# The first 35 microseconds of a linear-attention and MLP kernel: which queue loads what first, and in which order TensorE works

## The chip, the cores and the metric

The kernel runs on one core of a Trainium2 chip. A core has five engines that run at the same time, each in the order of its own instruction list: TensorE (PE, matrix products), VectorE (DVE), ScalarE (ACT), GpSimd (POOL) and SyncE (SP). Data comes from and goes to the chip's main memory by DMA transfers; SP, ACT and POOL issue them, each into a queue of its own, and 16 DMA engines carry all queues. Engines wait for each other and for transfers through semaphores. The metric is the time of one execution on the chip in microseconds (us); the median of three runs before the change is 657.64 us (657.43 to 659.58).

## The reference

Inputs are q, k and v of shape (4, 8, 768, 64) (batch, heads, positions, width of a head), a decay `lam` for each head, and the weights `w_in` (512 x 2048) and `w_out` (2048 x 512). The first half is linear attention with decay, in blocks of positions; the second half is an MLP with the activation h - tanh(h):

```python
intra = np.einsum('bhic,bhjc->bhij', qb, kb) * Dmask[None]
intra = np.einsum('bhij,bhjd->bhid', intra, vb)
inter = np.einsum('bhid,bhde->bhie', qb * lam_pow[None], kv_state)
out[:, :, sl] = intra + inter
kv_state = lam_block[None, :, None, None] * kv_state + np.einsum('bhsd,bhse->bhde', kb_dec, vb)
...
x = np.ascontiguousarray(attn_out.transpose(0, 2, 1, 3)).reshape(B * S, H * D)
h = x @ w_in
g = h - np.tanh(h)
return (g @ w_out).astype(np.float32)
```

`Dmask` holds `lam ** (i - j)` for i >= j and 0 otherwise, and `kb_dec` is k times `lam ** (block - 1 - position)`.

## The kernel before

The kernel works through the 768 positions in six groups of 128 positions (`NG`, `BLK`), each group with all four batches, so that one group makes 512 rows for the MLP. A *chunk* is one group of one batch: chunk (0, 2) is group 0, batch 2. For each chunk the kernel needs q, k and v as tiles of 128 positions by 8 heads by 64 (256 KB each).

The part around the change is group 0, where no state has to be read yet. For each of its four chunks:

- `load_natural` (line 153) issues the loads of q, k and v. All q go on SP's queue. Of group 0, the k of batches 0 and 1 goes on ACT's queue and everything else on POOL's (line 164).
- `att_transpose` (line 371) transposes q and k on TensorE (line 384, tiles `tp`), four products each, and ScalarE copies each result out of the accumulator memory (line 386, `qt` and `kt`).
- `att_scores` (line 393) makes the scores, eight products (line 400, tiles `sp`); VectorE multiplies them with the decay mask `whole` (line 407, tile `ss`, two instructions). `whole` is made once by eight scans on VectorE (line 110) out of `lam_all`, the decay of all heads, and the identity, which POOL writes.
- `att_decay` (line 428) scales k in place on VectorE (line 430).
- `first_out` (line 444) multiplies masked scores with v, eight products (line 451, tiles `op`). `first_tokens` (line 455) copies the outputs of two batches to `xt` on ScalarE (line 458): this is the input of the MLP.
- `kv_products` (line 432) and `first_state` (line 462) make the state that group 1 reads, from the scaled k and v of two batches.

The weights arrive as 64-bit words, in blocks. `load_weights` (line 254) issues the load of a raw block, `weights` (line 264) rounds the next ones (`round_block`, line 322): three passes on ScalarE (lines 332 to 334) and two on VectorE (lines 336, 337). Raw blocks have four buffers, so a block's load has to wait for the rounding of the block four places ahead of it. `ready["may"]` bounds how many raw blocks may be loaded so far; each `w_in` block has 512 KB, and blocks 2 and 3 of every four are loaded in two halves (line 250).

`up_plain` (line 887) is the first MLP product (tiles `h`, line 895). In the beginning it is used as an iterator, `unit`: `steps(unit, 2)` issues the next two of its steps, so that its products stand between the attention's.

`idle_products(n)` (line 358) issues n products of a tile of zeros into an unused bank of the accumulator memory. Their result is not used; they fill TensorE's time.

Order is written out by hand in this stretch: nearly every instruction is kept in program order (`tied`, `keep_in_program_order`), and the lines 969 to 1017 say which piece comes after which. `held(op, engines...)` (line 961) makes the next load on each of the named queues wait for `op`; what stands behind that load in the same queue waits with it. Before the change three places use it: loads of chunk (0, 2) wait for the masked scores of batch 0 (line 971), raw block 2 for the masked scores of batch 1 (line 978), and chunk (0, 3) with what follows for the first copy to `xt` (line 984).

In the built program each transfer of the hardware queues (SP and ACT) takes one of eight completion semaphores in turn, POOL's transfers have their own eight. A transfer waits, in its queue, until the earlier one with the same semaphore has landed.

Of the kernel before, what the change touches and what calls it, by code (L numbers as in the profile page):

```python
# [24 lines left out]
def kernel(  # L25
# [32 lines left out]
    nc = tc.nc  # L58
    B, H, S, D = q.shape
# [33 lines left out]
    lam_all = const.tile([128, H], F32)  # L93
    fwd = const.tile([128, NP, BLK], F32)
    nc.vector.memset(fwd[:, 0, :], 0.0)
    nc.gpsimd.dma_start(out=lam_all, in_=bass.AP(tensor=lam.tensor, offset=lam.offset, ap=[[0, 128], [1, H]]))
    make_identity(nc, ident)


# [53 lines left out]
    def load_natural(g, b, names):  # L153
        for name, src, bufs in (("q", q, 2), ("k", k, 3), ("v", v, 4)):
            if name in names:
                if (g, b, name) in ((0, 2, "q"), (0, 3, "q"), (0, 3, "k")):
                    x = opool.tile([128, H, D], F32, name=f"{name}_nat", tag="o")
                else:
                    x = (qpool if name == "q" else io).tile([128, H, D], F32, name=f"{name}_nat", tag=name, bufs=bufs)
                rows = src[b, :, ts(g, BLK), :].rearrange("h s d -> s h d")  # L160
                if name == "q":
                    parts = [(nc.sync, x, rows)]
                elif g == 0:
                    parts = [(nc.scalar if name == "k" and b < 2 else nc.gpsimd, x, rows)]
                else:
                    parts = [(nc.sync, x[ts(1 - t, HALF), 4:8], rows[ts(t, HALF), 4:8]) for t in range(2)]
                    parts.insert(0, (nc.sync, x[:, 0:4], rows[:, 0:4]))
                for eng, to, of in parts:
                    op = tc.keep_in_program_order(eng.dma_start(out=to, in_=of))  # L169
                    if begin.get(eng) is not None:  # L170
                        wait_for(op, begin.pop(eng))
                raw[g, b][name] = x
# [81 lines left out]
    def load_weights(n):  # L254

        while ready["loaded"] < min(n, ready["may"]):
            if moe_w_in.dtype != F32:
                raw64 = stage.tile([128, 2, 256], I64, name="raw64", tag="raw64", bufs=WAHEAD)
                block = blocks[ready["loaded"]]
                load_block(nc.gpsimd if ready["loaded"] in range(NU * KI, NU * KI + 4) else nc.sync, raw64, *block, True)  # L260
                wraw[ready["loaded"]] = raw64
            ready["loaded"] += 1
# [79 lines left out]

    for b in range(B):
        raw[0, b] = {}
    for b in (0, 1):
        load_natural(0, b, "qk")
    ready["may"] = 1
    load_weights(1)
    for b in (0, 1):
        load_natural(0, b, "v")  # L350
    ready["may"] = 2
    load_weights(2)
    at["loaded"] = B


# [2 lines left out]
    def idle_products(n, first=False):  # L358

        for _ in range(n):  # L360
            tied(not first, nc.tensor.matmul(out=idle[:, 0:128], lhsT=fwd[:, 0, :], rhs=fwd[:, 0, :], start=True, stop=True))
# [31 lines left out]
    def att_scores(g, bs):  # L393
        for b in bs:
            qt, kt, _ = tr[g, b]
            if g == 0:
                sp = [bank("sp", "att", 4).rearrange("s (p i) -> s p i", p=NP) for _ in range(2)]
                for p in range(NP):
                    for j in range(2):
                        tied(True, nc.tensor.matmul(out=sp[j][:, p, :], lhsT=kt[ts(j, 64), p, :],  # L400
                                                    rhs=qt[ts(j, 64), p, :], start=True, stop=True))
                if b % 2 == 0:
                    sc[0, "half"] = wst.tile([128, 8, 256], F32, name="ss", tag="w").rearrange(
                        "s (b j x) c -> s b j (x c)", b=2, j=2).rearrange("s b j (p i) -> s b j p i", p=NP)
                ss = sc[0, "half"][:, b % 2]
                for j in range(2):
                    op = tied(True, nc.vector.tensor_tensor(ss[:, j], sp[j], whole[:, j], op=AL.mult))
                sc[g, b] = ss
                continue

            sp = [bank("sp", "att", 4)[:, 0:6 * HALF].rearrange("s (x i) -> s x i", x=6) for _ in range(2)]
            for p in (0, 2, 1, 3):
                x, r = p % 2, p // 2
                for j in range(2):
                    kj, qj = kt[ts(j, 64), p, :], qt[ts(j, 64), p, :]

                    k0, k1 = (kj[:, ts(t if r == 0 or g >= GB else 1 - t, HALF)] for t in range(2))
                    tied(g != 1, nc.tensor.matmul(out=sp[j][ts(r, HALF), x:3 + p:2 + p - x, :], lhsT=k0,  # L418
                                                  rhs=qj.rearrange("d (t i) -> d t i", t=2), start=True, stop=True))
                    tied(g != 1, nc.tensor.matmul(out=sp[j][ts(1 - r, HALF), 2 + p, :], lhsT=k1,  # L420
                                                  rhs=qj[:, HALF:BLK], start=True, stop=True))
            ss = work.tile([128, 2, 6, HALF], F32, name="ss", tag="ss")
            for j in range(2):
                op = tied(g != 1, nc.vector.tensor_tensor(ss[:, j], sp[j], mask[:, j], op=AL.mult))
            sc[g, b] = ss
        return op

    def att_decay(g, b):
        kp = raw[g, b]["k"].rearrange("s (p j) d -> s p j d", j=2)
        return tied(g != 1, nc.vector.tensor_tensor(kp, kp, bwd if g > 0 else bwd_first, op=AL.mult))  # L430

    def kv_products(g, bs):

        kv = bank("kv", *(("yb", 1) if g >= GB else ("z", 1) if (g, bs) == (0, (0, 1)) else ("att", 4))).rearrange("d (b p e) -> d b p e", b=2, p=NP)
        for n, b in enumerate(bs):
            kd, vn = raw[g, b]["k"], raw[g, b]["v"]
            for p in range(NP):
                for j in range(2):
                    tied(g == 0, nc.tensor.matmul(out=kv[ts(j, 64), n, p, :], lhsT=kd[:, 2 * p + j, :],
                                                  rhs=vn[:, 2 * p + j, :], start=n == 0 and p == 0, stop=True,  # L440
                                                  skip_group_check=True))
        return kv

    def first_out(b):
        n, half = b % 2, b // 2
        if n == 0:
            reads[0, half] = [bank("op", "att", 4).rearrange("d (p b s) -> d p b s", p=2, b=2) for _ in range(2)]
        ops, ss, vn = reads[0, half], sc.pop((0, b)), raw[0, b]["v"]
        for p in range(NP):
            for j in range(2):  # L450
                tied(True, nc.tensor.matmul(out=out_dst(ops, n, p, j), lhsT=vn[:, 2 * p + j, :], rhs=ss[:, j, p, :],
                                            start=n == 0 and p % 2 == 0, stop=n == 1 and p % 2 == 1,
                                            skip_group_check=True))
# [507 lines left out]
    def held(op, *engines):  # L961
        begin.clear()
        begin.update({eng: op for eng in engines})

    def more_raw(n):
        ready["may"] = n
        load_weights(n)

    att_transpose(0, (0,))
    idle_products(3)  # L970
    held(att_scores(0, (0,)), nc.sync, nc.gpsimd)
    load_natural(0, 2, "qk")
    att_decay(0, 0)
    att_transpose(0, (1,))
    idle_products(2)
    first_out(0)
    att_decay(0, 1)
    held(att_scores(0, (1,)), nc.sync)
    more_raw(3)
    kv = kv_products(0, (0, 1))  # L980
    idle_products(2)
    weights(1)
    first_out(1)
    held(first_tokens(0)[0], nc.sync, nc.gpsimd)
    load_natural(0, 3, "qk")
    load_natural(0, 2, "v")
    more_raw(4)
    load_natural(0, 3, "v")
    ready["may"] = len(blocks)
    idle_products(6)  # L990
    unit = up_plain(0, [(i, c + 10 * a) for c in (11, 12) for i in range(KI) for a in range(2)])
    steps(unit, 2)
    weights(2)
    idle_products(4)
    att_transpose(0, (2,))
    steps(unit, 2)
    weights(3)
    att_scores(0, (2,))
    att_decay(0, 2)
    idle_products(6)  # L1000
    att_transpose(0, (3,))
    steps(unit, 2)
    weights(4)
    att_scores(0, (3,))
    first_out(2)
    att_decay(0, 3)
    idle_products(4)
    first_out(3)
    first_tokens(1)
    first_state((0, 1), kv)  # L1010
    steps(unit, 2)
    weights(5)
    steps(unit, 4)
    first_state((2, 3), kv_products(0, (2, 3)))
    weights(6)
    every(unit)
    weights(2 * KI)
# [177 lines left out]
```

## Time and profile before

| what | before |
|---|---|
| median of three runs | 657.64 us (657.43 to 659.58) |
| the profiled execution | 657.46 us |
| its span, first to last instruction | 655.7 us |
| TensorE products busy | 649.3 us (99%), 5782 instructions |
| TensorE weight loads busy | 595.9 us (91%) |
| VectorE busy | 470.2 us (72%) |
| ScalarE busy | 244.3 us (37%) |
| GpSimd busy | 206.0 us (31%) |
| DMA, mean over the span | 192 GB/s |
| DMA from 2 to 13 us | 255 GB/s, engines busy at a share of 1.02 |

The profile is of one execution; times in it count from the first instruction. A matrix product of 32-bit numbers shows as two records, so eight products of one kind read as x16. In the timeline a row is a run of like instructions: start, length, engine, line, tiles, and in square brackets the idle time of the engine just before it and what ended it. The chain of waits goes back from the last instruction of the program, at each step to what released it or to the instruction before it on its engine.

### The profile page before, as it was taken

Reading aid. Unit: us, or ns where it says so; the run is one execution under the profiler, and the core shown is the slowest. Engines: PE = TensorE matmul, PEld = TensorE weight load, DVE = VectorE, ACT = ScalarE, POOL = GpSimd, SP = SyncE. Lnnn points to the kernel's source line nnn. Section 1 sums busy time; section 2 is a strip of 40 time slices with the busy share of each in tenths; the row PEclk is TensorE's granted clock in tenths of the full one; section 3 lists DMA queues with packets and bytes.
Section 4 is the critical chain, followed back from the end, with each engine's and each line's share of the span. In section 5 each row is a group of like instructions: output and inputs, shape, how many; then the busy total and the mean of one; then the engine's idle time right before and its main releaser. Section 6 shows DMA issues by size and latency. Waiting matters only on the chain.

```text
span 655.7 us, 14869 instructions
## 1 busy us (share of the span) xinstructions
PE 649.3 (99%) x5782; PEld 595.9 (91%) x5782; DVE 470.2 (72%) x893; ACT 244.3 (37%) x485; POOL 206.0 (31%) x354
## 2 busy tenths in 40 slices
PE   8999999999999999999999999999999999999998
PEld 7888888888888999988999988999988899998897
DVE  4447989968878895678786668788468697466663
ACT  3576964622321223532223442213453223263210
POOL 2100125776133334202335302243411254400241
PEclk9999999999999999999999999999999999999999
DMA  7939977997858768957656967576867476621374
GB/s 194 246 113 214 240 227 209 387 277 222 183 129 218 219 190 246 217 103 184 198 182 219 240 127 161 149 235 196 208 158 153 123 259 219 228 69 33 85 250 163
DMA packets 154422, 125.78 MB, mean 192 GB/s; under 512 B 124928, under 2 KB 127232, under 8 KB 154352
## 3 DMA queue, kind: packets, MB, share of 16 engines
q0 software_dynamic: 27072, 88.04, 43.3%
q1 hardware_dynamic: 125200, 36.27, 25.6%
q8 instruction: 46, 0.75, 0.5%
q10 hardware_dynamic: 2080, 0.52, 0.4%
q14 instruction: 24, 0.20, 0.1%
HBM read 103.81 MB, written 20.97 MB: 190 GB/s over the span
## 4 chain that ended last, share of the span: by engine, by line
PE 80%; DMA 6%; issue 5%; SPq 4%; DVE 3%; POOL 1%; ACT 0%; POOLq 0%; DVEq 0%
PE y L601 14%; PE y L839 12%; PE zw L839 9%; PE h L895 7%; PE y L685 5%; PE z L601 5%; PE acc L925 4%; PE y L786 4%; PE w L786 4%; PE z L685 3%; SPq L181 2%; DMA q_blk<-in_q_dram 2%; SPq L169 2%; PE w L685 1%; PE sp L418 1%
## 5 line engine op out<-in xcount | busy, mean ns | idle before, releaser
L744 POOL DMA_DIRECT2D wb<-fine x148 | 79.9, 540 | 186.3 <-PE y L786 69.6
L843 ACT ACTIVATE q<-y 128x128 f32<-128x128 f32 x96 | 26.7, 278 | 142.8 <-PE y L839 141.9
L839 PE MATMUL y<-wb,g 128*128 128x128 f32 x456 | 60.2, 277 | 0.0
L895 PE MATMUL h<-xt,w 128*128 128x256 f32 x256 | 58.2, 383 | 0.3 <-DVE w L337 0.3
L839 PEld LDWEIGHTS y<-wb,g 128*128 128x128 f32 x456 | 55.1, 192 | 0.6
L895 PEld LDWEIGHTS h<-xt,w 128*128 128x128 f32 x256 | 47.4, 190 | 7.8 <-DVE w L337 1.3
L747 POOL DMA_DIRECT2D wb<-factors x44 | 23.7, 541 | 84.3 <-PE y L786 50.8
L609 ACT ACTIVATE th<-g 128x512 f32<-128x512 f32 x40 | 25.2, 630 | 66.5 <-DVE g L627 50.7
L601 PE MATMUL y<-xt,w 128*128 128x256 f32 x192 | 45.0, 379 | 0.0
L610 DVE TENSOR_TENSOR g<-g,th 128x512 f32<-128x512 f32 x40 | 27.6, 691 | 20.7 <-ACT th L609 20.7
L601 PEld LDWEIGHTS y<-xt,w 128*128 128x128 f32 x192 | 36.4, 190 | 5.1 <-ACT g L618 0.2
L839 PE MATMUL zw<-wb,g 128*128 128x128 f32 x304 | 40.3, 276 | 0.3 <-DMA wb<-fine 0.3
L601 PE MATMUL y<-tt,ws 128*128 128x256 f32 x160 | 37.8, 379 | 0.0
L601 PE MATMUL y<-tt,w 128*128 128x256 f32 x160 | 37.8, 379 | 0.0
L601 PE MATMUL z<-xt,ws 128*128 128x256 f32 x160 | 37.8, 379 | 0.0
L839 PEld LDWEIGHTS zw<-wb,g 128*128 128x128 f32 x304 | 37.0, 192 | 0.7 <-DVE tt L666 0.5
L786 PE MATMUL y<-wb,g 128*128 128x256 f32 x160 | 37.3, 379 | 0.0
L786 PE MATMUL w<-wb,g 128*128 128x256 f32 x160 | 35.3, 379 | 0.0
L786 PEld LDWEIGHTS y<-wb,g 128*128 128x128 f32 x160 | 30.4, 190 | 4.1
L786 PEld LDWEIGHTS w<-wb,g 128*128 128x128 f32 x160 | 30.4, 190 | 4.1
L601 PEld LDWEIGHTS z<-xt,ws 128*128 128x128 f32 x160 | 30.4, 190 | 4.1
L601 PEld LDWEIGHTS y<-tt,w 128*128 128x128 f32 x160 | 30.3, 190 | 4.2
(212 smaller groups left out, 1465.7 us busy)
## 6 DMA issues: line engine op xcount, KB each, us to landing
wb<-fine POOLq DMA_DIRECT2D x148, 256.0 KB, 3.6
wb<-factors POOLq DMA_DIRECT2D x44, 256.0 KB, 4.9
wb<-fine_in POOLq DMA_DIRECT2D x36, 256.0 KB, 4.1
raw<-in_moe_w_out_dram SPq DMA_DIRECT2D x12, 512.0 KB, 5.0
rest<-fine POOLq DMA_DIRECT2D x20, 256.0 KB, 4.3
raw<-in_moe_w_in_dram SPq DMA_DIRECT2D x8, 512.0 KB, 7.2
raw<-in_moe_w_in_dram SPq DMA_DIRECT2D x16, 256.0 KB, 6.2
fine<-f POOLq DMA_DIRECT2D x16, 256.0 KB, 4.8
```

The source lines that it names most:

```text
L169: op = tc.keep_in_program_order(eng.dma_start(out=to, in_=of))
L601: nc.tensor.matmul(out=t[:, m, :], lhsT=wt[:, kt, ts(m, 128)], rhs=x[:, kt, :], start=first and m == 0 and kt == 0, stop=kt == 1, skip_gro ...
L609: nc.scalar.activation(th, src, AF.Tanh)
L610: nc.vector.tensor_tensor(dst(c), src, th, op=AL.subtract)
L685: nc.tensor.matmul(out=dst[:, ts(u, 128)], lhsT=a, rhs=b, start=x in (1, 2, 5) and u == 0, stop=True, skip_group_check=True)
L744: nc.gpsimd.dma_start(out=t.rearrange("p m c -> p (m c)"), in_=fine[TWICE.index(n_), SUB.index(x_)].rearrange("p u c -> p (u c)"))
L747: nc.gpsimd.dma_start(out=t, in_=factors[XAT[FACT[n_][1]]][:, 2 * x_:2 * x_ + 2, :])
L786: nc.tensor.matmul(out=t[:, m, :], lhsT=a[:, u, kt, ts(m, 128)], rhs=wb[:, kt, :], start=first and u == 0 and m == 0 and kt == 0, stop=u = ...
L839: tied(x == STEPS[-1], nc.tensor.matmul(out=dst, lhsT=a[:, u, :], rhs=wb[:, ts(u, 128)], start=x in (1, 2) and u == 0, stop=u == NU - 1, s ...
L843: nc.scalar.activation(keep, dst, AF.Copy)
L895: tied(u == 0, nc.tensor.matmul(out=hm[c][:, m, :], lhsT=w1[u][:, i, a, ts(m, 128)], rhs=xt[0, t][:, i, :], start=m == 0 and i == 0, stop= ...
L925: nc.tensor.matmul(out=acc[n][:, r, :], lhsT=a[:, ts(r, 128)], rhs=b, start=kt == 0 and r == 0, stop=kt == KH - 1, skip_group_check=True)
```

## The change

- `lam` is loaded by SP, as its first transfer, and no longer by POOL.
- The v of batches 0 and 1 of group 0 goes on ACT's queue, behind the two k. The k of batch 2 goes on SP's queue.
- The loads of q and k of chunk (0, 2) and of raw block 2 stand directly behind the first loads, with no `held`. One `held` is left: chunk (0, 3), the v of batch 2 and raw block 3 wait for the masked scores of batch 0.
- The scores of batch 1 stand ahead of the outputs of batch 0, and the scaling of the k of batch 1 behind a weight block's rounding.
- The kv products of batches 0 and 1 stand behind the first step of `up_plain`, those of batches 2 and 3 earlier than before.
- Idle products: after the first eight, 3, 2, 2, 6, 4, 6, 4 before; 4, 4, 5, 6, 4, 6 after.
- The scores of batch 3 stand ahead of the rounding of weight block 3.

```diff
-    nc.gpsimd.dma_start(out=lam_all, in_=bass.AP(tensor=lam.tensor, offset=lam.offset, ap=[[0, 128], [1, H]]))
+    nc.sync.dma_start(out=lam_all, in_=bass.AP(tensor=lam.tensor, offset=lam.offset, ap=[[0, 128], [1, H]]))
...
-                    parts = [(nc.scalar if name == "k" and b < 2 else nc.gpsimd, x, rows)]
+                    parts = [(nc.scalar if b < 2 else nc.sync if (b, name) == (2, "k") else nc.gpsimd, x, rows)]
...
-    for b in (0, 1):
-        load_natural(0, b, "qk")
-    ready["may"] = 1
-    load_weights(1)
-    for b in (0, 1):
-        load_natural(0, b, "v")
-    ready["may"] = 2
-    load_weights(2)
+    for names in ("qk", "v"):
+        for b in (0, 1):
+            load_natural(0, b, names)
+        if names == "qk":
+            ready["may"] = 2
+            load_weights(2)
+    load_natural(0, 2, "qk")
+    ready["may"] = 3
+    load_weights(3)
     at["loaded"] = B
...
-    def more_raw(n):
-        ready["may"] = n
-        load_weights(n)
-
     att_transpose(0, (0,))
-    idle_products(3)
+    idle_products(4)
     held(att_scores(0, (0,)), nc.sync, nc.gpsimd)
-    load_natural(0, 2, "qk")
+    load_natural(0, 3, "qk")
+    load_natural(0, 2, "v")
+    load_natural(0, 3, "v")
+    ready["may"] = 4
+    load_weights(4)
+    ready["may"] = len(blocks)
     att_decay(0, 0)
     att_transpose(0, (1,))
-    idle_products(2)
+    idle_products(4)
+    att_scores(0, (1,))
     first_out(0)
+    idle_products(5)
+    weights(1)
     att_decay(0, 1)
-    held(att_scores(0, (1,)), nc.sync)
-    more_raw(3)
-    kv = kv_products(0, (0, 1))
-    idle_products(2)
-    weights(1)
     first_out(1)
-    held(first_tokens(0)[0], nc.sync, nc.gpsimd)
-    load_natural(0, 3, "qk")
-    load_natural(0, 2, "v")
-    more_raw(4)
-    load_natural(0, 3, "v")
-    ready["may"] = len(blocks)
+    first_tokens(0)
+    unit = up_plain(0, [(i, c + 10 * a) for c in (11, 12) for i in range(KI) for a in range(2)])
     idle_products(6)
-    unit = up_plain(0, [(i, c + 10 * a) for c in (11, 12) for i in range(KI) for a in range(2)])
     steps(unit, 2)
     weights(2)
-    idle_products(4)
+    kv = kv_products(0, (0, 1))
     att_transpose(0, (2,))
     steps(unit, 2)
     weights(3)
     att_scores(0, (2,))
     att_decay(0, 2)
-    idle_products(6)
+    idle_products(4)
     att_transpose(0, (3,))
     steps(unit, 2)
+    att_scores(0, (3,))
     weights(4)
-    att_scores(0, (3,))
     first_out(2)
     att_decay(0, 3)
-    idle_products(4)
+    idle_products(6)
     first_out(3)
     first_tokens(1)
     first_state((0, 1), kv)
     steps(unit, 2)
+    kv = kv_products(0, (2, 3))
     weights(5)
+    first_state((2, 3), kv)
     steps(unit, 4)
-    first_state((2, 3), kv_products(0, (2, 3)))
     weights(6)
```

## The prediction, made before the changed kernel ran

> **What bounds the kernel now.** I read the table of cores and slices first: TensorE is busy 99% of the span, so only time taken from TensorE's own sequence can move the end. The diff touches the first 35 us alone, and the instruction lists of the two programs agree from there on, so I read the chain of waits of that stretch next:
>
> ```profile
> 2.44 8.79 DMA v_nat<-in_v_dram
> 11.22 0.14 issue
> 11.36 1.09 PE op L451 x16
> 12.45 1.09 PE sp L400 x16
> 13.54 1.08 PE kv L439 x32
> 14.62 0.64 PE idle L361 x4
> 15.27 1.02 PE op L451 x16
> 16.29 1.53 PE idle L361 x12
> 17.83 1.73 PE h L895 x8
> 19.55 0.89 PE idle L361 x8
> 20.45 0.87 PE tp L384 x8
> ...
> 28.28 1.09 PE sp L400 x16
> 29.37 1.02 PE op L451 x16
> 30.39 1.09 PE idle L361 x8
> 31.48 1.02 PE op L451 x16
> 32.51 2.57 PE h L895 x11
> ```
>
> The columns are start, length and work. Until 11.22 us the first v transfer sets the pace. From 11.36 to 32.51 TensorE runs without a hole; what is not useful there is idle products (line 361), which have a fixed count. So a gain can come from what precedes 11.36, or from fewer idle products. The timeline of TensorE and VectorE before it:
>
> ```profile
> 4.63 1.08 PE L384 MATMUL tp<-ident,q_nat 128*128 128x128 f32 x4
> 7.30 1.16 PE L400 MATMUL sp<-qt,kt 64*128 64x128 f32 x16
> 8.40 0.66 PE L384 MATMUL tp<-ident,q_nat 128*128 128x128 f32 x4
> 9.61 0.63 PE L384 MATMUL tp<-ident,k_nat 128*128 128x128 f32 x4 [0.55 <-DMA k_nat<-in_k_dram]
> 11.36 1.09 PE L451 MATMUL op<-ss,v_nat 128*64 128x128 f32 x16 [0.67 <-DMA v_nat<-in_v_dram]
> ...
> 7.09 2.63 DVE L110 TENSOR_TENSOR_SCAN whole<-lam_all,ident 128x128 f32<-128x128 f32 x8 [6.08 <-DMA lam_all<-in_lam_dram]
> 9.64 1.26 DVE L407 TENSOR_TENSOR ss<-sp,whole 128x512 f32<-128x512 f32 x2
> ```
>
> Two holes, 0.55 us for the second k and 0.67 us for the first v. VectorE is late as well: the scans start only at 7.09, when lam has landed, and the masked scores end at 10.90, just before the v. Third view, the transfers (issue, then us to landing): q of chunk 0 issued 0.74, 3.7; k 0.74, 4.4; second q 1.25, 6.7; second k 1.27, 8.2; lam 1.25, 5.7; raw weight blocks 1.86 and 2.71, 8.0 and 10.7; v 2.44 and 3.35, 8.8 and 9.2. From 2 to 13 us the DMA engines are busy at a share of 1.02 with 255 GB/s: they are full.
>
> **The change part by part.**
>
> *lam on SyncE.* Removes one issue from POOL (0.65 us); identity is ready earlier, which nobody waits for. lam is now the first issue on SP. Its landing there is not in the trace. Bounds: 3.3 us (a lone q at 10.93) and 10.7 us (a raw block in the crowd). I take 3.7, the q issued at the same moment from the same queue: landing near 4.5, scans done near 7.2. They leave the path, and the masked scores can follow the first score products. At the upper end lam lands at 11.4, the scores' mask ends near 15.3, and the first outputs slip about 3 us.
>
> The price: q, q and the first raw block each go one issue later on SP. An issue there lasts 0.44 to 0.81 in this stretch; I take 0.5. The first transpose began at 4.63, with its q landed at 4.5; with q half a microsecond later and now behind the k (before, the later of the pair landed at 5.1), it begins near 5.2. Idle products still run to 4.63, then a hole of 0.55. Transposes, copies and the copy's wait follow as before, so score products start at 7.85 instead of 7.30: +0.55. Bounds: 0.1 (q not late, only the fourth idle product) and 0.8 (the longest issue).
>
> *First v's on ScalarE's queue, behind both k's.* Two more issues of 0.5 to 0.7 on ACT, from 2.0 to 3.2; its table load (1.28) then ends near 4.5, and its first copy begins at 5.75 in the trace and later after the change: hidden by 1.2 us. POOL loses 1.8 us of issue that nothing waits for. Landing: ACT's queue landed the second k at 9.5. Half of 255 GB/s moves 262 KB in 2.06 us, so an estimate is 11.5 for the first v and 13.6 for the second. Upper bound: the 4.3 us between the two k's, again twice: 13.8 and 18.1. I take the estimate, since SP's queue, the only other one left, cannot be given more than its share for long. The outputs need them at 12.1 and 14.4 (below): met by 0.6 and 0.8.
>
> A row speaks against this move: as v on POOL's queue, 0.53 MB took 192 packets and 19.3% of the engines in 2 to 13 us; as k on ACT's queue 0.52 MB took 2080 packets and 21.5%. That is 0.24 us more engine time for the two v's, inside the margins. The Trainium skill, DMA: Bandwidth & Descriptors, Why small descriptors are slow (HBM only), gives 27% overhead for a 256-byte descriptor. By that the estimate would be 0.57 us for the pair (27% of 19.3% of 11 us); the trace shows less than half, and the sum would stay the same.
>
> *Third chunk and third raw block not held.* In the built program hardware-queue transfers take eight completion semaphores in turn, and one waits until the transfer eight places earlier landed. So the second raw block now waits on SP for the first k (5.1 instead of 2.7), and behind it in order stand the third q and k (waiting for lam and the first q), the third raw block's halves (second k and second q) and the fourth q (first v, and the first masked scores). Nothing is late: ScalarE needs the second raw block at 16.9 (before), the transposes need the third chunk at 20. POOL's third k becomes SP's, and POOL's v issues follow the first masked scores (near 10.4) rather than 16.8. These loads land earlier than needed in both kernels, so I cost them at nothing; without that cover each microsecond late would count fully.
>
> *Order on TensorE and VectorE.* Scores of the second batch go ahead of the first outputs; the kv products move from 13.5 to behind the first h group, in place of four idle products; idle products after the first score products are 4, 5, 6, 4, 6 instead of 2, 2, 6, 4, 6, 4. On VectorE the second scores' mask goes ahead of the second decay, and the fourth chunk's mask ahead of a weight block's rounding. The decay waits only for the kv products, now near 18.7; that rounding ends near 30.8 and is needed at 31.8: covered. The second kv sum moves ahead of eight h products, same length.
>
> **The sum**, with the chain's own lengths. Scores 7.85 to 8.95; transpose of q to 9.40; transpose of k from 9.55 (k landed 9.5) to 9.99; four idle products 0.99 (mean of 0.89 and 1.09), 10.98; scores 1.09, 12.07; outputs 1.05 (v landed 11.5, mask done 10.4), 13.12; five idle 1.31, 14.43; outputs 1.02, 15.45; six idle 1.53 and an issue, 17.00. The h group started at 17.83 before. Then h 1.73, kv 1.08, transposes 0.87, h 1.73, scores 1.09, idle 0.99, transposes 0.87, h 1.73, scores 1.09, outputs 1.02, idle 1.53, outputs 1.02: 14.75, which gives 31.75 where before had 32.51. From there the work and its order are the same: **-0.75 us**. Later stops (0.26 us at 59.9, and the stretch from 102 to 123 where the chain runs on VectorE) follow TensorE's own results through ScalarE and VectorE, so they shift along.
>
> The profiled execution took 657.46 (span 655.7 and 1.8 around it), 0.18 under the median of 657.64. 657.46 - 0.75 = 656.7.
>
> **Rivals.**
>
> 1. *TensorE's clock opens later: slower.* The timeline shows passes 0.21 us apart from 1.06 on (idle products, both first transposes) and 0.11 from 6.8 on, so full speed came 5.7 us after TensorE began, with no hole between; the granted clock in the table of stretches reads 1.00 from 2 us on and misses this. The hole of 0.55 at 4.63 is new. If the count starts again at its end, full speed comes at 10.9, and 4.2 us run at half speed: +2.1, 658.8. It decides from a delay of 1.5 us on (0.75 lost). Against it: a hole of half a microsecond is small beside 5.7. The Trainium skill, TensorE: Matmul & The Clock Gate, section Part 1: The HAM clock gate, has a free-running window of about 3.4 us that must be busy. By that one more window at half speed would be an estimate of +1.7 us, 658.4; the trace has one opening and cannot tell.
>
> 2. *v's late on ACT's queue.* At the upper bound (13.8, 18.1) the second outputs wait 3.7 us: 660.4; half way 658.5. It turns into a loss when the second v lands after 15.2. For it: the second k took 8.2 us there. Against: POOL's packets, which competed at its end, are gone.
>
> 3. *The gain stays in the beginning*, because a later stop is not set by TensorE: 657.5. Against it: none of the stops named above is ended by a transfer.
>
> 4. *q not late*, and the holes are worth their start-to-start lengths (0.7 and 0.8): -1.5, 656.0.
>
> **How the numbers follow.** Forecast 0.55, clock 0.2, late v's 0.1, gain lost 0.1, better case 0.05. I say 656.7, its own range 656.0 to 657.4. The whole range takes the better case and 0.4 for the scatter of the runs, 655.6, and the clock's case with as much, 659.2; it leaves out the worst v's and double trouble. 0.3% of 657.64 is 1.97 us, about what a measurement of this kernel can tell from no change. Faster than 655.7: only beyond the better case, 0.05. Slower than 659.6: clock and v's together, or v's near the bound, 0.08. Same 0.87.
>
> **What would show it.** In the profile after: lam landed before 5 and scans done before the first masked scores; first transpose near 5.2; no hole above 0.3 before the outputs; the first main h group near 17.0 and the one at 32.51 near 31.75. Wrong if passes stay 0.21 apart beyond 8 us, if outputs are released by a v transfer, or if the stage from 32 to 130 us changes its length.

## The result: 0.37% slower, and the profile after

The changed kernel took 659.62 us (median of 14 runs, 658.88 to 661.93) against 657.57 us for the kernel before (14 runs, 656.83 to 659.58). The ratio is 1.0037, with a 95% interval of 1.0026 to 1.0048. The prediction said 656.7, within 655.6 to 659.2: wrong in sign, and outside its range. The profiled execution of the changed kernel took 660.45 us, 0.83 above its own median, with a span of 658.6; before had 657.46 and 655.7. The two profiles therefore differ by 2.99, the medians by 2.05.

The chain of waits of the changed kernel from 0 to 36 us, in the form shown before (start, length, work):

```profile
1.19 6.09 DMA q_nat<-in_q_dram
7.28 0.14 issue
7.42 1.94 PE tp L385 x8
9.36 1.71 PE idle L362 x8
11.06 2.01 PE sp L401 x16
13.07 1.06 PE tp L385 x8
...
21.01 1.73 PE h L896 x8
...
33.47 1.54 PE idle L362 x12
35.01 1.02 PE op L452 x15
```

A q now sets the pace of the beginning, where before it was the first v at 11.22. It was issued only 0.45 us later than before, but it took 6.1 us instead of 3.7 and landed at 7.28. The timelines of TensorE, VectorE, ScalarE and SP say what went with it (times from the first instruction, idle time before the row in brackets):

```profile
7.42 1.09 PE L385 MATMUL tp<-ident,q_nat 128*128 128x128 f32 x4 [2.58 <-DMA q_nat<-in_q_dram]
10.99 2.08 PE L401 MATMUL sp<-qt,kt 64*128 64x128 f32 x16
4.77 2.63 DVE L110 TENSOR_TENSOR_SCAN whole<-lam_all,ident 128x128 f32<-128x128 f32 x8 [3.77 <-DMA lam_all<-in_lam_dram]
1.87 4.87 ACTq L169 DMA_DIRECT2D v_nat<-in_v_dram  x2
6.77 1.28 ACT L387 ACT_TABLE_LOAD   x1 [6.77 <-issue]
8.54 0.60 ACT L387 ACTIVATE qt<-tp 128x512 f32<-128x512 f32 x1 [0.49 <-PE tp L385]
2.28 4.13 SPq L245 DMA_DIRECT2D raw<-in_moe_w_in_dram  x2
```

The new hole before the first transpose is 2.58 us, not 0.55. The scores take 2.08 us, where the same sixteen records took 1.16 before: TensorE still runs at half speed there. The scans did become early (4.77 instead of 7.09), and nobody could use it. ScalarE spent 4.87 us issuing two transfers.

From landmark to landmark, the start of each piece on TensorE:

| | before | predicted | after |
|---|---|---|---|
| first transpose | 4.63 | 5.2 | 7.42 |
| first score products | 7.30 | 7.85 | 10.99 |
| their end, next transpose starts | 8.40 | 8.95 | 13.01 |
| first main h group | 17.66 (17.83 in the chain) | 17.00 | 20.85 |
| the h group at 32.5 | 32.44 (32.51 in the chain) | 31.75 | 35.96 |
| from the scores' end to that group | 24.04 | 22.80 | 22.95 |

The last row is the part that the new order was to shorten, and it did, by 1.09 us. The row above it is the net: +3.52, because the scores ended 4.61 later. These 4.61 are 2.79 for the late q, 0.92 for score products at half speed, and 0.90 between transposes and scores, where eight idle records ran 1.91 at half speed and before six ran 1.01; two of the eight are the fourth idle product of the new order. After the beginning the delay goes along: VectorE's instructions are 3.49 late at 438 us of the kernel before, for example; by 441 us 0.53 of it have come back, and the span ends 2.9 longer.

### The profile page after: what moved, and what is told of

Same layout as the page of the kernel before. It is cut to its first block, busy times and chain, and to the rows that moved or that the text cites. A ratio compares the mean times of both kernels' runs of the same rounds, so it can differ in the third digit from the quotient of the medians.

```text
span 658.6 us, 14874 instructions
## 1 busy us (share of the span) xinstructions
PE 651.1 (99%) x5786; PEld 597.5 (91%) x5786; DVE 470.3 (71%) x893; ACT 244.0 (37%) x485; POOL 202.8 (31%) x350
## 3 DMA queue, kind: packets, MB, share of 16 engines
q10 hardware_dynamic: 4160, 1.05, 0.9%
## 4 chain that ended last, share of the span: by engine, by line
PE 94%; DVE 3%; DMA 1%; issue 1%; ACT 0%; SPq 0%; DVEq 0%; ACTq 0%
PE y L602 17%; PE y L840 13%; PE zw L840 10%; PE h L896 8%; PE y L686 7%; PE z L602 6%; PE y L787 5%; PE w L787 5%; PE acc L926 4%; PE z L686 3%; PE w L686 2%; PE sp L419 2%; PE kv L440 2%; PE op L511 2%; PE op L482 1%; PE tp L385 1%
## 5 line engine op out<-in xcount | busy, mean ns | idle before, releaser
L610 ACT ACTIVATE th<-g 128x512 f32<-128x512 f32 x40 | 25.2, 630 | 66.5 <-DVE g L628 50.7
```

Of the source, the lines that this page charges most:

```text
L610: nc.scalar.activation(th, src, AF.Tanh)
```

## The experiments

They ask three things: what made q late, what the two v's cost on ScalarE's queue, and whether the unheld loads were as free as the prediction said. All three parts of the load change turned out to cost something with the others out of the way, so it took both "one part undone" and "one part alone" to see it. The unheld loads never ran in the old order of work; they were measured together with the new one.

### lam's place in the queue

One part undone: lam back on POOL, all else as in the changed kernel.

```diff
-    nc.sync.dma_start(out=lam_all, ...)
+    nc.gpsimd.dma_start(out=lam_all, ...)
```

> The changed kernel with the load of lam back on POOL; all else as changed. Theory A (lam's transfer at the head of SP's queue holds the first q back): the first q lands before 5.2 us, the first transpose starts near 4.7, passes are 0.11 us apart from about 6.8, and the gain of the new order (1.15 us measured between the scores and the main h group) stays: about 656.4 us, 1.1 under the kernel before. Rival B (the two v's on ACT's queue crowd out SP's q): the first q still lands near 7.3 and the time is about 659.6 us.

One part alone: the kernel before, with lam first on SP and nothing else changed.

```diff
-    nc.gpsimd.dma_start(out=lam_all, ...)
+    nc.sync.dma_start(out=lam_all, ...)
```

> The kernel before with lam as SP's first load and nothing else changed. Theory A: the first q lands near 7.3 us, the clock opens near 13, the scores of batch 0 end 4.7 us later than before; the two holes of 0.55 and 0.67 vanish in that delay, so about 3.5 us slower, 660 to 661 us. Rival B: the first q lands near 5 us and the time stays at 657.6 us or rises by at most 0.5.

With lam on POOL, q landed at 4.8 and the first transpose began at 4.93. With lam alone on SP, q landed at 7.0 and the first transpose began at 7.13. So lam's place decides the landing of q, in both orders of work. By itself it made the kernel slower: 659.01, ratio 1.0024 [1.0014, 1.0035], which is 1.6 us and not the 3.5 expected. But taking it out of the change did not help the total: 660.03, 1.0038 [1.0026, 1.0050]. Something else stood behind it (next part).

The table of stretches from 2.0 to 4.5 us (columns: length, busy time of PE, weight loads, DVE, ACT and POOL, granted clock, busy share of the DMA engines, GB/s), first of before:

```profile
2.00:4.50 2.50, 2.50 (x14) 2.50 (x12) 0.00 (x0) 1.28 (x1) 2.17 (x4) 1.00 1.10 241
```

The same of the changed kernel:

```profile
2.00:4.50 2.50, 2.50 (x14) 2.50 (x12) 0.00 (x0) 0.00 (x0) 0.00 (x0) 1.00 0.35 76
```

And of lam alone:

```profile
2.00:4.50 2.50, 2.50 (x14) 2.50 (x12) 0.00 (x0) 1.16 (x1) 1.39 (x2) 1.00 0.36 77
```

The last two columns are the finding. While lam (4 KB, in 128 pieces of 32 bytes) is on its way at the head of SP's queue, the DMA engines move 76 GB/s instead of 241, and the first k on the *other* queue suffers as well (landed at 5.84 instead of 5.13). The first 13 us of the changed kernel in 40 slices of 0.325 us:

```profile
GB/s 0 0 0 0 0 1 1 1 27 65 92 134 131 170 288 290 288 274 221 217 217 216 219 217 217 220 227 235 251 284 319 353 384 391 373 363 353 329 290 268
```

And of the kernel before:

```profile
GB/s 0 0 0 0 0 18 143 221 184 279 288 288 284 206 158 119 130 199 210 232 296 310 299 280 336 375 387 306 290 277 277 246 246 265 258 284 198 226 258 280
```

The changed kernel reaches 280 GB/s in the slice that starts at 4.55, about when lam lands (4.67); the kernel before reaches 279 at 2.9. Why so small a transfer idles the engines is not in these traces; that it does is. Its pieces are small, and all 128 read the same 32 bytes of memory (the access pattern in the diff of the change has a step of 0); no run parts the two.

A third run is the changed kernel with both v back on POOL and lam on SP, but behind the two q:

```diff
-    nc.sync.dma_start(out=lam_all, ...)
...
-    scans(range(NP), ident)
...
     for names in ("qk", "v"):
         for b in (0, 1):
             load_natural(0, b, names)
         if names == "qk":
+            tc.keep_in_program_order(nc.sync.dma_start(out=lam_all, ...))
             ready["may"] = 2
             load_weights(2)
+    scans(range(NP), ident)
```

> As the first of these (v's on POOL), with lam on SP's queue behind both q's instead of on POOL. If lam's place ahead of q is the cost: first q near 4.6 us, lam lands between 5 and 8, scores of batch 0 near 7.4, about 656.4 us. If lam's small pieces hold up the DMA engines wherever it stands in a hardware queue: second q and second k land one or two us later than before (8.0 and 9.5), a hole before the second pair of transposes, 657.5 to 658.5 us.

Now q landed at 4.56 and the stretch from 2.0 to 4.5 is full (share 1.06, 233 GB/s). So position counts, not presence. But lam then lands at 9.16, 7.3 us after its issue, and the mask takes the place of q. VectorE's scans and TensorE's second score products of this run:

```profile
9.26 2.63 DVE L109 TENSOR_TENSOR_SCAN whole<-lam_all,ident 128x128 f32<-128x128 f32 x8 [8.25 <-DMA lam_all<-in_lam_dram]
12.62 1.16 PE L401 MATMUL sp<-qt,kt 64*128 64x128 f32 x16 [1.83 <-DVE ss L408]
```

This kernel took 660.58, 1.0044 [1.0032, 1.0056], more than either side of its expectation. A hole of 1.83 us is not all of it: in its records the clock falls to half from 13.85 to 17.26. Its median is also higher than the landmark (35.23 for the h group at 32.5) suggests beside the changed kernel's 35.96; its runs lie between 659.55 and 661.38.

### The two v's on ScalarE's queue

Undone in the changed kernel (lam stays first on SP), and alone in the kernel before:

```diff
-  nc.scalar if b < 2 else nc.sync if (b, name) == (2, "k") else nc.gpsimd
+  nc.scalar if name == "k" and b < 2 else nc.sync if (b, name) == (2, "k") else nc.gpsimd
...
-  nc.scalar if name == "k" and b < 2 else nc.gpsimd
+  nc.scalar if b < 2 else nc.gpsimd
```

> The changed kernel with the v's of batches 0 and 1 back on POOL; lam stays SP's first. Theory A: the first q still lands near 7.3 us, the time is that of the changed kernel, 659.6 us, within 0.5. Rival B: the first q lands near 5 us and the time falls to about 656.5 us.

> The kernel before with the v's of batches 0 and 1 on ACT's queue and nothing else. Theory C: the issue of the second v lasts until about 6.9 us, the table load until 8.2, the first copy starts at 8.2 instead of 5.75, scores of batch 0 near 9.3 instead of 7.3, and the first outputs wait for the first v until about 13.2 instead of 11.3: about 2 us slower, 659.5 us. Rival: ScalarE is free by 4.5 us, scores at 7.3, time within 0.5 of the kernel before.

Undone, with lam first: q at 7.1, 659.61, 1.0032 [1.0020, 1.0044], nothing gained. Its profile still has the h group of 32.5 at 34.81, 1.15 ahead of the changed kernel's, and TensorE's timeline shows why:

```profile
10.75 1.16 PE L401 MATMUL sp<-qt,kt 64*128 64x128 f32 x16
```

The scores run at full speed here. After nearly the same hole (2.44 us, to 7.28, beside 2.58, to 7.42) the clock records have full speed from 10.58 on, in the changed kernel from 13.11. So some of the half speed above is the luck of the one execution that was profiled, which was also 0.83 above its median (last section).

Alone: 659.57, 1.0031 [1.0019, 1.0043], a loss of 2 us with q in time (4.6). ScalarE's timeline of the v's alone:

```profile
2.01 4.98 ACTq L169 DMA_DIRECT2D v_nat<-in_v_dram  x2
7.02 1.28 ACT L386 ACT_TABLE_LOAD   x1 [7.02 <-issue]
8.31 0.60 ACT L386 ACTIVATE qt<-tp 128x512 f32<-128x512 f32 x1
```

and TensorE's there:

```profile
9.45 2.08 PE L400 MATMUL sp<-qt,kt 64*128 64x128 f32 x16 [2.49 <-ACT kt L386]
```

The third issue on this queue (the first v) took from 2.01 to 3.51, the fourth from 3.54 to 6.99; in the changed kernel 1.87 to 4.63 and 4.66 to 6.74. During an issue ScalarE can do nothing else, so its table load, and behind it the first copy of a transpose, slipped from 5.75 to 8.31. TensorE stood 2.49 us for that copy. Lam undone alone could not help for this reason: there the v's held the first copy until 8.18, and TensorE waited 2.29.

Is it bytes or the number of pieces that holds the issuing engine? A further run leaves the v's on POOL and puts the first two raw weight blocks on ACT's queue, in the same places of the queue but with twice the bytes in larger pieces:

```diff
-  load_block(... else nc.sync, raw64, *block, True)
+  load_block(... else nc.scalar if ready["loaded"] < 2 else nc.sync, raw64, *block, True)
```

> The kernel before with the first two raw weight blocks on ACT's queue behind the two k's, where e6 had the two v's: the third and fourth load there now have 512 KB each in 256 pieces of 2 KB, instead of 256 KB in 1024 pieces of 256 bytes. If the number of pieces waiting in the queue is what holds ScalarE at the issue: both issues take below 1 us each, table load done by 5, first copy at 5.75 as in the kernel before, time within 0.7 of it. If bytes, or the third and fourth transfer as such, hold it: issue until 7 us or later, first copy after 8.2, about 2 us slower.

The page's table of DMA queues counts packets and MB of ACT's queue (q10): 2080 and 0.52 with two k, 4160 and 1.05 with two k and two v, and in this run:

```profile
q10 hardware_dynamic: 2624, 1.57, 0.9%
```

So a k or v is 1040 packets and a raw block 272. ScalarE's timeline in this run:

```profile
2.02 2.16 ACTq L245 DMA_DIRECT2D raw<-in_moe_w_in_dram  x2
4.21 1.28 ACT L386 ACT_TABLE_LOAD   x1 [4.21 <-issue]
5.50 0.60 ACT L386 ACTIVATE qt<-tp 128x512 f32<-128x512 f32 x1
```

Twice the bytes hold ScalarE 2.16 us instead of 4.98, and the first copy is in time. The number of packets, not bytes, is the larger part. It is not all: the first of these two issues still took 1.50 us, as the first v had, where below 1 was expected, and the second 0.62. In the kernel before the same block took 0.81 in the same third place of SP's queue (up to 1.30 in the other runs without lam ahead of it). Why ACT's third issue is held whatever it brings stays open. This kernel took 656.92 beside 657.89, 0.9984 [0.9974, 0.9994], a small gain that its profile does not explain: its h group at 32.5 came at 32.95, 0.5 *later* than before, in an execution (657.95) that was the longest of its ten. That, too, stays open.

### Both back, and what the unheld loads cost

Lam on POOL and the v's on POOL, by the first diff and the first half of the diff for the v's together: what is left of the change are the unheld loads, the k of batch 2 on SP, and the new order.

> The changed kernel with lam back on POOL and the v's of batches 0 and 1 back on POOL; order of work, third chunk and raw block as changed. Theory C (two causes, each enough by itself: lam ahead of q in SP's queue, and ScalarE held at the issue of its fourth load until 6.8 us): first q near 4.6, first copy on ScalarE near 5.8, scores of batch 0 near 7.4, main h group near 16.9 and the one at 32.5 before near 31.5, so about 1 us under the kernel before, 656.4 us. Rival D (the new order or the loads that are no longer held cost as well): 657.4 us or more, the h groups at 17.7 and 32.5 or later.

q landed at 4.7, the first copy began at 5.89, the scores ended at 8.20, and the first main h group began at 16.62, before the predicted 17.00. And yet the kernel took 659.34, 1.0034 [1.0017, 1.0051]. TensorE's timeline of this run:

```profile
16.62 1.89 PE L896 MATMUL h<-xt,w 128*128 128x256 f32 x8
26.68 0.63 PE L385 MATMUL tp<-ident,q_nat 128*128 128x128 f32 x4 [2.15 <-DMA q_nat<-in_q_dram]
34.51 1.78 PE L896 MATMUL h<-xt,w 128*128 128x256 f32 x7
```

and SP's:

```profile
4.03 4.94 SPq L169 DMA_DIRECT2D k_nat<-in_k_dram  x1
9.01 5.07 SPq L250 DMA_DIRECT2D raw<-in_moe_w_in_dram  x2
14.21 0.52 SPq L169 DMA_DIRECT2D q_nat<-in_q_dram  x1
```

The fourth q is issued at 14.21 and lands at 26.54, 12.3 us later. In the kernel before it was issued at 16.52 and landed at 21.77. My reading is that the third chunk and the third raw block, no longer held, take the DMA engines first, together with POOL's loads, of which the k of batch 3 is here released at 11.47 instead of 16.79. The DMA engines lost nothing: from 2 to 13 us they moved 259 GB/s beside 255, and from 13 to 26 us 212 at a share of 1.12 beside 193 at 0.86. What came late was overtaken. SP's issues stretch as ScalarE's did: 4.94 us for one k, which POOL had issued before. The third raw block came late as well, as ScalarE's timeline of this run shows:

```profile
25.18 0.66 ACT L332 ACTIVATE w<-raw 128x512 f32<-128x512 f32 x1 [3.82 <-DMA raw<-in_moe_w_in_dram]
```

If the raw block ahead of the fourth q is what delays it, moving that q ahead should free it:

```diff
-    ready["may"] = 3
-    load_weights(3)
...
     load_natural(0, 3, "qk")
+    ready["may"] = 3
+    load_weights(3)
```

> As the run with lam and the v's back on POOL, and the third raw block loaded behind the fourth chunk's q instead of ahead of it. If the raw block ahead of that q was the third cause: the fourth q lands by 20 us instead of 26.5, the hole of about 2.3 us before the last pair of transposes is gone, they start near 24.4, and the h group of 32.5 us starts near 31.5: 656.4 us, 1 under the kernel before. If not (POOL's three loads or the third k fill the queues): hole and time stay, about 659.3 us.

The fourth q landed at 20.72 and its transposes had no hole. Then a weight block was missing. TensorE's timeline of this run:

```profile
24.18 0.60 PE L383 MATMUL tp<-ident,q_nat 128*128 128x128 f32 x4
27.95 1.99 PE L894 MATMUL h<-xt,w 128*128 128x256 f32 x8 [2.73 <-DVE w L337]
```

and ScalarE's, which rounds that block, shows for what:

```profile
25.23 0.66 ACT L332 ACTIVATE w<-raw 128x512 f32<-128x512 f32 x1 [4.05 <-DMA raw<-in_moe_w_in_dram]
```

The third raw block is as late as in the run above (25.23 beside 25.18); there it stood hidden behind a q that was later still. What overtook them can be read from the runs together, by the second half of that block. In the three where SP issued it before POOL's first load was let go (the changed kernel, lam undone, lam third), it landed between 18.2 and 20.6, and the fourth q behind it between 21.1 and 21.5. In the five where POOL was ahead (v's undone, both back, q ahead, and the two runs of the next part), it landed from 22.1 on, at 25.2 in this run, and a fourth q behind it between 25.9 and 27.1. So POOL's loads, let go as soon as the first masked scores are done, fit as the ones that overtake; no run moved them alone. The h group at 32.5 came at 34.55, beside 34.51 in the run above. Its runs scatter from 658.24 to 665.74, median 661.30, 1.0056 [1.0037, 1.0074]; its one profile, of an execution of 659.33, cannot show what the longer ones had.

### Idle products, as a test of the clock and as time to save

The clock's part: 16 idle products ahead of the first transpose instead of 8, in the changed kernel, so that TensorE is busy while the late q is on its way.

```diff
-    idle_products(8, True)
+    idle_products(16, True)
```

> The changed kernel with 16 instead of 8 idle products ahead of the first transposes, so that TensorE works until about 7.3 us. If the late clock is a cost of its own: the first q lands near 7.3 us as in the changed kernel, but passes are 0.11 us apart from about 6.8, and transposes (1.94 to 0.87), idle products (1.71 to 0.99) and scores (2.01 to 1.09) of batch 0 give back about 2.5 us: 657.1 us. If the late q alone is the cost: 659.6 us.

q landed at 7.5, and what followed ran at full speed. TensorE's timeline of this run:

```profile
7.65 0.63 PE L385 MATMUL tp<-ident,q_nat 128*128 128x128 f32 x4 [0.88 <-DMA q_nat<-in_q_dram]
18.44 1.89 PE L896 MATMUL h<-xt,w 128*128 128x256 f32 x8
```

The first main h group came at 18.44 instead of 20.85, 2.41 earlier, although the first transpose was 0.23 later. But 0.81 of it went into a hole before the last transposes (the fourth q landed at 27.0), the h group at 32.5 gained 1.41, and the time did not improve: 660.08, 1.0041 [1.0029, 1.0053]. The landmark was right and the time, 657.1, a miss. Some of it was lost later: VectorE's lead over the changed kernel is still about 1.4 us up to 430 us, then 0.80, and 0.23 at 545 us. What takes it there was not followed up.

Less idle work, with lam and the v's back on POOL (six places, in order):

```diff
-    idle_products(4), (4), (5), (6), (4), (6)
+    idle_products(4), (3), (2), (5), none, (2)
```

> As the first of these (lam and v's on POOL), with the idle products after the first eight cut from 4, 4, 5, 6, 4, 6 to 4, 3, 2, 5, none, 2. If TensorE's fixed list sets the pace of this stretch: 13 products of 0.255 us less, 3.3 us, down to what VectorE and the loads allow: about 654 us. If the loads set it (the fourth chunk's q and k): 655.5 us or more, with a hole before the last pair of transposes.

The first main h group came at 15.69, and the hole for the fourth q grew to 3.57 us (it landed at 26.0); the h group at 32.5 came at 34.23. 658.54 (655.72 to 661.29), 1.0016 [1.0000, 1.0032]: time that is freed ahead of a late transfer becomes waiting, and the clock fell to half behind that hole as well (27.16 to 30.57).

### The order of work alone

Last, the kernel before with all its loads and its three held places, and only the order and the idle products of the change:

```diff
     att_transpose(0, (0,))
-    idle_products(3)
+    idle_products(4)
     held(att_scores(0, (0,)), nc.sync, nc.gpsimd)
     load_natural(0, 2, "qk")
     att_decay(0, 0)
     att_transpose(0, (1,))
-    idle_products(2)
-    first_out(0)
-    att_decay(0, 1)
+    idle_products(4)
     held(att_scores(0, (1,)), nc.sync)
     more_raw(3)
-    kv = kv_products(0, (0, 1))
-    idle_products(2)
+    first_out(0)
+    idle_products(5)
     weights(1)
+    att_decay(0, 1)
     first_out(1)
...
```

> The loads of the kernel before, with the changed order of work on TensorE, VectorE and ScalarE. If the order is the gain that I worked out and every loss comes from the loads: main h group near 16.7, the h group of 32.5 near 31.5, no hole before the transposes, 656.4 us. If the order itself costs: 657.5 us or more.

And the same with the shorter idle work, with the six counts 4, 3, 2, 5, none, 2 as in the diff of the part before:

> As the one before, with idle products after the first eight cut from 4, 4, 5, 6, 4, 6 to 4, 3, 2, 5, none, 2. If the loads of the kernel before arrive in time for it: 13 products of 0.255 us less, down to the waits for the copies: h group of 32.5 near 29, 654 us. If not, holes before the last transposes or outputs and 655.5 to 656.5 us.

TensorE's timeline of the order alone:

```profile
16.63 1.89 PE L895 MATMUL h<-xt,w 128*128 128x256 f32 x8
24.37 0.60 PE L384 MATMUL tp<-ident,q_nat 128*128 128x128 f32 x4
31.74 1.99 PE L895 MATMUL h<-xt,w 128*128 128x256 f32 x8
```

No row from 4.75 to 31.74 has a wait in brackets. The h group stands 0.70 ahead of before's 32.44, and the kernel took 656.66 (656.08 to 657.73) against 657.49: 0.9983 [0.9974, 0.9992]. With the shorter idle work two loads become the next to wait for; TensorE's timeline of that run:

```profile
8.77 0.63 PE L384 MATMUL tp<-ident,q_nat 128*128 128x128 f32 x4 [0.88 <-DMA q_nat<-in_q_dram]
22.61 0.66 PE L384 MATMUL tp<-ident,q_nat 128*128 128x128 f32 x4
30.27 1.99 PE L895 MATMUL h<-xt,w 128*128 128x256 f32 x8 [1.05 <-DVE w L337]
```

The second q comes 0.88 late and a rounded weight block 1.05 late, but the h group is still 2.17 ahead of before. This is the fastest version, ahead of both kernels: 655.49, 0.9970 [0.9957, 0.9984]. Put side by side (h group at 32.5 on TensorE; "full speed from" by the clock records, which the run with lam alone lacks; each ratio is against the kernel before on the same chip):

| kernel | first q landed | first copy on ScalarE | full speed from | h group at 32.5 | median us | ratio |
|---|---|---|---|---|---|---|
| before | 4.5 | 5.75 | 6.74 | 32.44 | 657.57 | |
| after | 7.3 | 8.54 | 13.11 | 35.96 | 659.62 | 1.0037 |
| lam alone | 7.0 | 8.25 | | 34.29 | 659.01 | 1.0024 |
| v's alone | 4.6 | 8.31 | 5.82, then 12.64 | 34.56 | 659.57 | 1.0031 |
| unheld loads and order | 4.7 | 5.89 | 5.63 | 34.51 | 659.34 | 1.0034 |
| order alone | 4.6 | 5.87 | 7.01 | 31.74 | 656.66 | 0.9983 |
| order alone, less idle work | 4.6 | 5.38 | 3.90 | 30.27 | 655.49 | 0.9970 |

## Why the prediction was wrong, step by step

**"lam on SyncE": right.** I took a landing near 4.5 and scans done near 7.2; measured 4.67 and 7.40.

**"q half a microsecond later": failed, the largest single term.** I counted the issue that lam adds on SP, 0.5, with bounds of 0.1 and 0.8. The issue was 0.39; q came 2.8 later, because transfers behind lam, and those beside it, hardly move until it has landed. My bounds came from issue lengths alone. They left out that the transfer ahead can slow down the ones behind. The rows to bound it were there: 3.3 us for a lone q and 6.7 for a q in the crowd.

**"Two more issues of 0.5 to 0.7 on ACT": failed.** Measured 2.76 and 2.08 (1.50 and 3.45 for the v's alone). The cover of 1.2 us that I named was real, and 2.49 more was needed when the v's moved alone. In the changed kernel the late transposes hide this: ScalarE was free at 8.05 and then waited 0.49 for them. The trace of before had no row of a third transfer of 1040 packets in a hardware queue whose first two had not landed; I carried over the length of the first issues. The Trainium skill, DMA: Bandwidth & Descriptors, Issuing engines are not separate DMA queues, says that issuing on several engines saves only the sequencer's time for initiating, "which is usually small relative to the DMA itself". These runs do not agree for a busy queue: initiating took 4.8 to 5.1 us of the engine for two transfers, the first of which, in the changed kernel, landed 8.7 us after its issue.

**"Lands earlier than needed in both kernels, so I cost them at nothing": failed.** The condition I wrote beside it, "each microsecond late would count fully", is what happened: with nothing else against it, the fourth q was 4.8 us later than before and TensorE stood 2.15 for it, in the trimmed version 3.57; ScalarE stood 3.82 for the third raw block. In the changed kernel itself this does not show: its late scores let POOL's loads go only at 14.71, behind the third raw block (13.51) and the fourth q (14.42), which landed at 21.5, and TensorE, 3 us late, needed it only at 28.59.

**The order of work: right.** Predicted 31.75, measured 31.74 with the loads left alone, and 656.66 against the 656.7 forecast. Part of this agreement is chance: I predicted a later beginning (+0.55) and a shorter middle (-1.3). The run has +0.42, of which nothing is a late q (4.6), and -1.12 from the scores' end on.

**Rival 1, the clock opens later: it did, at a hole five times as large.** I took a hole of 0.55 and priced the loss at +2.1. The hole was 2.58; the clock records put full speed at 13.1 instead of 6.74, and the half speed cost up to 1.82 (0.90 and 0.92 above). That full speed came 5.7 us after the hole, as I had written, is chance: with the v's back on POOL it came 3.3 us after a like hole. The count does not start at the end of a hole (last section). The run with sixteen idle products removes the half speed and puts the first main h group 2.41 earlier. **Rival 2, late v's:** in the changed kernel the first v landed at 10.6, well ahead of my 11.5, and no output waited for a v. With the q's in time, though, it landed at 12.1 (v's alone) and 13.1 (lam back on POOL), where my sum has the first outputs at 12.07: had all else gone as forecast, they would have stood up to a microsecond for it. What hurt was their issue, which I had priced and dismissed. **Rival 3** fell: the gain of the order alone reached the end. **Rival 4,** "q not late", was the reverse of what happened.

The three costs do not add. Each alone puts the h group about 2 us late (1.85 for lam, 2.12 for the v's, 2.07 for the unheld loads with the order's gain inside; 2.77 beside the order alone). Together they are 3.52, since a late q hides a late ScalarE, and late scores hold back POOL's loads, which else go ahead of the third raw block and the fourth q. That is why undoing lam or the v's, one at a time, moved the time by less than 0.5 us, and why only the order alone settled what the order is worth. The changed kernel with only its loads held again was not run.

## What to carry to other kernels

Moving a load to another queue has three prices besides the issue's usual length: what the transfer does to those behind it, how long the issue holds the engine when many packets already wait in that queue, and whose place in full DMA engines it takes. Price them from a row in the same state of the queue, or give the bound by the slowest row there is. When several parts each hide the others, test parts alone as well as undone, and keep an order change and a load change apart. And a profile is one execution: where its clock opened moved a landmark by a microsecond here.

## What the runs showed of the hardware

- A 4 KB transfer of 32-byte pieces at the head of SP's queue left the DMA engines at 76 GB/s for 2.5 us (241 without it). All four kernels with lam there show it (73 to 77); third in that queue (233) or on POOL's (236) it did not.
- An issue on ACT or SP took 0.4 to 0.8 us in the first 29 us of the kernel before, and up to 5 us behind transfers of 1040 packets that had not landed (ACT's v 2.76 and 2.08, SP's third k 4.94). Not each one did: with both back, SP's third q took 0.60 behind two q's that had not landed, and the k after it the 4.94. SP's first raw block took 3.28 instead of 0.81 when the queue stood behind lam.
- The granted clock closed after some holes of about 2 us. With a hole of 2.29 us at 7.0 to 9.3 it fell to half from 10.95 to 14.36, with one of 2.49 from 9.23 to 12.64, with 1.83 from 13.85 to 17.26, with 3.57 from 27.16 to 30.57: always for 3.41 us. The run with lam back on POOL, in the table of stretches (seventh value: the granted clock):

```profile
11.00:14.30 3.30, 3.30 (x19) 3.07 (x19) 1.40 (x3) 2.96 (x5) 2.19 (x3) 0.50 1.36 222
14.40:18.00 3.60, 3.60 (x50) 3.19 (x50) 2.75 (x5) 0.00 (x0) 0.38 (x1) 1.00 1.11 179
```

  The hole cost 2.29 us and the half speed after it was paid on top. The Trainium skill, TensorE: Matmul & The Clock Gate, Part 1: The HAM clock gate, has a free-running window of 3413 ns; the closed stretches agree. It puts the fall after an idle window of about that length; here holes of 1.83 to 2.49 us were followed by one, while holes of 2.15 and 2.73 us in other runs were not.

- What decided was the idle time inside one fixed stretch, not the length of the hole. In the four runs above it fell one, two or six times 3.41 us after it had opened. So I cut each run into stretches of that length, counted from the opening in its clock records (lam alone and sixteen idle products left none), and take TensorE's busy time in each (the second value). First the run with lam third, whose clock fell at the end of this stretch, then the run with both back, whose clock did not, since its hole of 2.15 lies in two stretches:

```profile
10.43:13.85 3.42, 1.59 (x22) 1.30 (x22) 3.31 (x9) 2.10 (x4) 0.49 (x1) 1.00 1.20 306
22.70:26.11 3.41, 1.83 (x22) 1.51 (x18) 0.23 (x1) 0.93 (x2) 0.00 (x0) 1.00 1.09 224
26.11:29.52 3.41, 2.67 (x15) 2.29 (x16) 2.54 (x5) 3.17 (x6) 0.00 (x0) 1.00 0.77 252
```

  TensorE stood 1.83 us in the first of these, and 1.78, 2.27 and 2.33 in the other three stretches that ended in a fall. It stood 1.58 and 0.74 in the second and third, and 1.70 at most in any stretch of these runs, from the opening to 36 us, that did not end in one. The clock first opened at the end of a stretch with up to 0.57 us idle, and not with 0.72 or more. In the changed kernel the stretches to 6.28 and 9.70 had 1.45 and 1.13 idle, so it opened with the next, at 13.11. With the v's back on POOL the stretch from 7.17 to 10.58 began only 0.11 ahead of the first transpose, and it opened at 10.58. Where the stretches lie differs from execution to execution: full speed began anywhere from 3.90 to 7.02 us in the runs whose first q was in time.
